# Routing the conversion of the first and second layers' weight chunks through PSUM, in a fused attention and two-layer MLP kernel

## The chip, the cores and the metric

One core of a Trainium2 chip runs the whole kernel in one launch. The metric is the device time of one execution in microseconds (us). The kernel before took 1555.38 us in the median of three runs (1552.1 to 1557.77).

## What is computed

Packed attention, then two gated MLPs one after the other, over 4608 tokens of width 512:

```
p_packed = softmax(scale * p @ k.T) @ v            # 32 packed rows per head
x  = softmax(scale * q @ p_packed.T) @ p_packed    # 8 batches, 8 heads, 576 tokens, head width 64
h  = x @ w_in;    x2  = (h * cos(h)) @ w_out       # 512 -> 2048 -> 512
h  = x2 @ w2_in;  out = (h * tanh(softplus(h))) @ w2_out
```

The four weight matrices arrive as 8-byte floats. The engines work on 4-byte ones, so each weight chunk of 128 rows by 512 columns is loaded as pairs of 4-byte words and put together on the chip.

## The kernel before, in words

The work runs in 16 token tiles of 288 tokens. Each tile goes through 16 steps, one per 128 columns of the hidden layer: 256 steps in all, then the second MLP in five blocks. In a step n (loop at line 911) the kernel traces, in this order: `l1(n)`, six TensorE matmuls that make a 128x288 piece of h in a PSUM bank; matmuls of background units; `l2(n-3)`, twelve matmuls into four accumulator banks; the chain h*cos(h), which is ScalarE's rounding (L802), VectorE's range reduction (L804), VectorE's clamp (L805), ScalarE's sine (L811), VectorE's product with h (L812, the last reader of the bank), ScalarE's rounding to the high half (L819) and GpSimd's low half (L822); and then VectorE, ScalarE and DMA work of background units, entered in tables by step (`at_pe`, `at_ew`, `at_ld`).

PSUM has eight banks. Four are the accumulators `acc0` to `acc3` (line 105), each with one buffer; they are first needed by `l2(0)`. Four are a ring (line 102) which `l1`, the folding of packed rows into the first layer's weights (`w_unit`, matmuls at L491, evacuation at L510 and L511), and the score and transpose banks of the attention share.

`conv` (line 408) converts a weight chunk. Its parts are: the load of the raw words (L424, on SP's queue); `c1`, in which ScalarE turns the high word into a scaled float (L436, a Prelu) and VectorE shifts the low word (L437); `c2`, in which VectorE merges the two (L441); `c3`, which writes the chunk to DRAM for later tiles (L446) or rounds the high half on ScalarE (L450); and `c4`, the low half on GpSimd (L455). All operands lie in SBUF. It serves three kinds of chunks: 16 of the first layer (`w_load`, line 462, placed at line 708 by `W0_STEP`, steps -5 to 10), 16 of the second layer's weights of the first MLP (`wo1_unit`, line 517, steps 0 to 15, with a raw buffer that is one of two), and 16 of the second MLP (`pre2`, much later).

A planner with its own costs of each instruction orders every engine's queue when the kernel is built. It goes by the order of tracing, by due times (`tc.high_priority`: l1 by 150, the chain by 200, the weight folding by 400) and by when it expects a buffer to be free. Each engine then executes its queue strictly in order.

Of the kernel before, what the change touches and what calls it, by code (L numbers as in the profile page):

```python
# [8 lines left out]
F32 = mybir.dt.float32  # L9
F32R = mybir.dt.float32r  # L10
I32 = mybir.dt.int32
AF = mybir.ActivationFunctionType
ALU = mybir.AluOpType
# [74 lines left out]
def build(tc, q, k, v, p, w1i, w1o, w2i, w2o, out):  # L88
    nc = tc.nc
    ctx = ExitStack()  # L90
    with ctx:
        wpool = ctx.enter_context(tc.tile_pool(name="wpool", bufs=1))
        psum = ctx.enter_context(tc.tile_pool(name="psum", bufs=1, space=bass.MemoryType.PSUM))
# [4 lines left out]
        def nm(s):  # L98
            cnt[0] += 1
            return f"{s}_{cnt[0]}"  # L100
# [3 lines left out]

        def accs():
            return [psum.tile([128, 512], F32, tag=f"acc{j}", bufs=1, name=nm(f"acc{j}")) for j in range(4)]

        def wo_tile(shape, dt):
            return wpool.tile(shape, dt, tag="wo", bufs=16, name=nm("wo"))

        def wab_tile(ab, shape, dt):
            return wpool.tile(shape, dt, tag="wa" if ab == 0 else "wb", bufs=4, name=nm("wab"))

        def ld_tile(shape):
            return wpool.tile(shape, F32, tag="ld", bufs=LD_BUFS, name=nm("ld"))
# [19 lines left out]
        def tmp_tile(shape):  # L135
            return tp.tile(shape, F32, tag="tmp", bufs=TMP_BUFS, name=nm("tmp"))
# [268 lines left out]
                (None, s7),  # L405
            ]

        def conv(src, shape, dst, save, wide=False, st=None):
            st = {} if st is None else st

            def load():
                if wide == "wo":
                    r = wo_tile([128, 512, 2], I32)
                elif wide:
                    w = wab_tile(1, [128, 2048], I32)
                    r = w[:, :1024].rearrange("p (f t) -> p f t", t=2)
                    st["t"], st["m"] = w[:, 1024:1536], w[:, 1536:].bitcast(F32)
                else:
                    r = tp.tile([128, 512, 2], I32, tag="raw", bufs=2, name=nm("raw"))
                n = shape[-1] if len(shape) == 3 else 512  # L420
                if len(shape) == 3:
                    nc.sync.dma_start(r.rearrange("p (a f) t -> p a (f t)", f=n), src.bitcast(I32))
                else:
                    ins = nc.sync.dma_start(r.rearrange("p f t -> p (f t)"), src.bitcast(I32))  # L424
                    last_w[0] = getattr(ins, "ins", ins)
                st["r"] = r

            def c1():
                r = st["r"]
                if wide == "wo":  # L430
                    w = wo_tile([128, 1024], I32)
                    st["t"], st["m"] = w[:, :512], w[:, 512:].bitcast(F32)
                elif not wide:
                    st["t"] = tp.tile([128, 512], I32, tag="tmp", bufs=TMP_BUFS, name=nm("cvt"))
                    st["m"] = tmp_tile([128, 512])
                nc.scalar.activation(st["m"], r[:, :, 1].bitcast(F32), AF.Prelu, scale=2.0**-112, alpha=2.0**32)  # L436
                nc.vector.tensor_scalar(st["t"], r[:, :, 0], 29, None, ALU.logical_shift_right)  # L437

            def c2():
                mi = st["m"].bitcast(I32)  # L440
                nc.vector.scalar_tensor_tensor(mi, mi, 3, st["t"], ALU.logical_shift_left, ALU.bitwise_or)  # L441

            def c3():
                if save is not None:
                    d = dram.tile([128, 512], F32, name=nm("ws"))
                    nc.sync.dma_start(d, st["m"])  # L446
                    save(d)
                if dst is not None:
                    hi, _ = st["x"] = dst()
                    nc.scalar.copy(hi, st["m"])  # L450

            def c4():
                if dst is not None:
                    hi, lo = st["x"]
                    nc.gpsimd.tensor_tensor(lo, st["m"], hi, ALU.subtract)  # L455

            return load, [c1, c2, c3, c4]

        W1 = {}
        w1s = {}  # L460

        def w_load(fg, hp, fresh=False):
            st = {}
            if fresh:
                load, cs = conv(
                    w1i[128 * hp : 128 * hp + 128, 512 * fg : 512 * fg + 512],
                    [128, 512],
                    None,
                    lambda d: w1s.__setitem__((fg, hp), d),
                    "wo" if fg == 0 else True,  # L470
                    st,
                )
                return st, load, cs[:-1]

            def load():
                st["m"] = ld_tile([128, 512])
                nc.sync.dma_start(st["m"], w1s[(fg, hp)])

            return st, load, []

        def w_unit(bs, fg, g, ms):
            st = {}

            def pe():
                for b in bs:
                    st[b] = ring()

                def head(b, l):
                    h = PERM[b % 2][l]
                    r = 64 * (h % 2)  # L490
                    return nc.tensor.matmul(  # L491
                        st[b][32 * l : 32 * l + 32],
                        PK[(b, g)][r : r + 64, 32 * l : 32 * l + 32],
                        ms[h // 2]["m"][r : r + 64],
                        start=True,
                        stop=True,
                    )

                todo = sorted(((b, l) for b in bs for l in range(4)), key=lambda x: (-(PERM[x[0] % 2][x[1]] // 2), -x[0]))
                ins = head(*todo[0])  # L500
                with tc.issue_after(getattr(ins, "ins", ins)), tc.high_priority(offset=HP_W):
                    for x in todo[1:]:
                        head(*x)

            def ew():
                for b in bs:
                    w = W1.get((b, fg))
                    if w is None:
                        w = W1[(b, fg)] = wab_tile(b % 2, [128, 2, 2, 512], F32R)
                    nc.scalar.copy(w[:, g, 0], st[b])  # L510
                    nc.vector.tensor_tensor(w[:, g, 1], st[b], w[:, g, 0], ALU.subtract)  # L511

            return pe, ew
# [3 lines left out]
        def wo1_unit(ft):  # L517
            def dst():
                w = wo_tile([128, 2, 512], F32R)
                WO[(1, ft)] = w  # L520
                return w[:, 0], w[:, 1]

            return conv(w1o[128 * ft : 128 * ft + 128, :], [128, 512], dst, None)

        WST = {}
        w2s = {}
# [1 line left out]
        def pre2(key, src, shape):  # L528
            return conv(src, shape, None, lambda d: w2s.__setitem__(key, d))
# [131 lines left out]
        def at_pe(n, f):  # L661
            bg_pe.setdefault(n, []).append(f)

        def at_ew(n, f):
            bg_ew.setdefault(n, []).append(f)

        def at_ld(n, f):
            bg_ld.setdefault(n, []).append(f)
# [37 lines left out]
        place(stages, [PRO + Q0_T + i for i in range(2)] + [PRO + Q0 + i for i in range(6)], HP_PRO)  # L706
        ms = {}
        for j in range(16):
            ms[j], load, cs = w_load(j // 4, j % 4, True)
            n = W0_STEP[j]  # L710
            at_ld(n - W0_LD if j >= 4 else PRO + W0E[j], load)
            for i, f in enumerate(cs):
                at_ew(n - 3 + i, f)
            if j % 2:
                pe, ew = w_unit((0,), j // 4, j % 4 // 2, (ms[j - 1], ms[j]))
                at_pe(n, pe)
                at_ew(n, ew)
        for ft in range(16):
            load, cs = wo1_unit(ft)
            n = ft + WO_OFF  # L720
            at_ld(n - 2, load)
            for i, f in enumerate(cs):
                at_ew(n + i // 2, f)
# [6 lines left out]
        for j in range(16):  # L730
            ms[j], load, _ = w_load(j // 4, j % 4)
            n = W01[0] + int(W01[1] * j)
# [12 lines left out]
        for j, n in enumerate(I_AT):  # L745
            w, c = divmod(j, 2)
            src = w2i[256 * c : 256 * c + 256, 256 * w : 256 * w + 256].rearrange("(a p) f -> p a f", p=128)
            load, cs = pre2((w, c), src, [128, 2, 256])
# [4 lines left out]
        for pair in range(3):  # L753
# [9 lines left out]
            for j in range(16):  # L763
                ms[j], load, _ = w_load(j // 4, j % 4)
                n = n0 + W_POS[pair][0] + int(W_POS[pair][1] * (j // 2 * 2 + 1))
# [5 lines left out]
        for t in range(1, NT):  # L771
            n = Q_N[t - 1]
# [52 lines left out]
        acc = {}  # L825

        def l2(n):
            t, s = divmod(n, NF)
            if s == 0:
                acc[t] = accs()  # L830
            w, gh = WO[(1, s)], hst[n]["gh"]
            for dc in range(4):
                o = 128 * dc
                mm3(acc[t][dc][:, :TT], w[:, 0, o : o + 128], w[:, 1, o : o + 128], gh[:, 0], gh[:, 1], s == 0, s == NF - 1)
            del hst[n]
# [75 lines left out]
        for n in range(NA + LAG_A):  # L911
# [7 lines left out]
            m = n - LAG_A  # L919
# [280 lines left out]
```

## Time and profile before

| what | value |
|---|---|
| median of 3 runs | 1555.38 us (1552.1 to 1557.77) |
| the profiled execution, its own time | 1555.48 us |
| its span, first to last instruction | 1552.9 us |
| mean granted TensorE clock | 0.989 of 2.4 GHz |
| busy: TensorE matmul, VectorE, ScalarE, GpSimd | 1475.9, 1117.8, 883.9, 639.2 us |
| DMA moved | 300.75 MB, mean 194 GB/s |

The table gives averages over the whole span. The span has parts with different limits, so the rows further down cut out the start of the kernel, where the weight chunks of the first MLP are converted. In the rows PE is TensorE, DVE VectorE, ACT ScalarE, POOL GpSimd and SP the queue that issues DMAs; L441 is line 441 of the kernel.

### The profile page before, as it was taken

The numbers are of one execution on the slowest core, as the hardware profiler recorded it, in microseconds if no ns is written. First come the engines' busy times: TensorE is split into PE (matmuls) and PEld (weight loads), VectorE is DVE, ScalarE is ACT, GpSimd is POOL, SyncE is SP. The second block draws the span as 40 slices with busy tenths as digits, with TensorE's granted clock in tenths as the row PEclk, the third lists the DMA queues.
The fourth block names the chain that finished last, engine by engine and source line by source line (L and its number), as shares of the span: only waits on it lengthen the run. The fifth ranks groups of instructions, "written<-read, shape, count | busy, mean of one in ns | idle before, by whom it ended". The sixth has DMA issues, their size and how long they took to land.

```text
span 1552.9 us, 28652 instructions
## 1 busy us (share of the span) xinstructions
PE 1475.9 (95%) x9728; PEld 1278.3 (82%) x9728; DVE 1117.8 (72%) x2082; ACT 883.9 (57%) x1838; POOL 639.2 (41%) x634
## 2 busy tenths in 40 slices
PE   3789999999999999999999999999999999999998
PEld 1567778788987898788999887888889898888997
DVE  4896666777776877678675878678668857766756
ACT  3675767666667677667665455344443534454443
POOL 0462333245643544627754666223522622352102
PEclk9899999999999999999999999999999999999999
DMA  9889676436648457533313767668868877877887
GB/s 293 283 214 226 170 184 161 123 101 176 186 122 225 139 152 195 163 107 104 104 49 98 259 217 241 193 196 242 266 212 235 298 223 219 244 205 221 241 257 202
DMA packets 247377, 300.75 MB, mean 194 GB/s; under 512 B 104384, under 2 KB 129472, under 8 KB 247232
## 3 DMA queue, kind: packets, MB, share of 16 engines
q1 hardware_dynamic: 246432, 298.73, 66.1%
q8 instruction: 77, 1.26, 0.3%
q14 instruction: 68, 0.56, 0.1%
q10 hardware_dynamic: 800, 0.20, 0.1%
HBM read 242.22 MB, written 56.62 MB: 192 GB/s over the span
## 4 chain that ended last, share of the span: by engine, by line
PE 50%; DVE 6%; ACT 3%; issue 2%; DMA 2%; POOL 1%; SPq 0%; DVEq 0%; ACTq 0%; POOLq 0%
PE acc L146 9%; PE acc L147 9%; PE acc L145 9%; PE ps L145 8%; PE ps L147 8%; PE ps L146 8%; DVE r L805 1%; ACT r L811 1%; DVE r L812 1%; DVE r L804 1%; DMA raw<-in_moe_w_in_dram 1%; DVE wab L897 1%; ACT wab L896 1%; PE ps L491 0%; DMA tst<-wt 0%
## 5 line engine op out<-in xcount | busy, mean ns | idle before, releaser
L822 POOL TENSOR_TENSOR gh<-r,gh 128x288 fp32r<-128x288 f32 x256 | 214.9, 847 | 334.3 <-ACT gh L819 231.7
L146 PE MATMUL acc<-gh,wo 128*128 128x288 f32 x1024 | 301.5, 301 | 2.2 <-POOL gh L822 1.7
L147 PE MATMUL acc<-gh,wo 128*128 128x288 f32 x1024 | 298.2, 298 | 0.0
L955 POOL TENSOR_TENSOR gh<-t,gh 128x512 fp32r<-128x512 f32 (+1 forms) x108 | 144.2, 1340 | 351.5 <-ACT gh L954 290.7
L145 PE MATMUL acc<-gh,wo 128*128 128x288 f32 x1024 | 273.7, 304 | 2.1 <-ACT gh L819 1.9
L145 PEld LDWEIGHTS acc<-gh,wo 128*128 128x128 f32 x1024 | 181.2, 190 | 34.6 <-issue 11.9
L146 PE MATMUL acc<-gh,T 128*128 128x512 f32 (+1 forms) x560 | 207.0, 371 | 2.2 <-DVE gh L955 1.7
L145 PE MATMUL ps<-wab,ws 128*128 128x512 f32 (+1 forms) x560 | 206.0, 369 | 1.8 <-ACT gh L954 0.8
L146 PEld LDWEIGHTS acc<-gh,wo 128*128 128x128 f32 x1024 | 194.1, 190 | 15.9 <-issue 9.5
L146 PE MATMUL ps<-wab,ws 128*128 128x512 f32 (+1 forms) x560 | 206.4, 369 | 0.0
L147 PE MATMUL ps<-wab,ws 128*128 128x512 f32 (+1 forms) x560 | 205.4, 369 | 0.0
L147 PE MATMUL acc<-gh,T 128*128 128x512 f32 (+1 forms) x560 | 205.1, 369 | 0.0
L147 PEld LDWEIGHTS acc<-gh,wo 128*128 128x128 f32 x1024 | 194.2, 190 | 5.8 <-issue 5.6
L955 DVE TENSOR_TENSOR gh<-wo,gh 128x512 fp32r<-128x512 f32 (+1 forms) x160 | 128.7, 810 | 81.7 <-ACT gh L954 81.3
L811 ACT ACTIVATE r<-r,halfpi 128x288 f32<-128x288 f32 x256 | 136.3, 535 | 83.9 <-DVE r L805 81.6
L145 PE MATMUL acc<-gh,T 128*128 128x512 f32 (+1 forms) x560 | 181.9, 369 | 0.6 <-DMA T<-tst 0.5
L145 PE MATMUL ps<-aT,wab 128*128 128x288 f32 x512 | 159.7, 312 | 22.7 <-DVE r L812 16.5
L812 DVE TENSOR_TENSOR r<-r,ps 128x288 f32<-128x288 f32 x256 | 114.5, 449 | 73.3 <-ACT r L811 72.5
L802 ACT ACTIVATE ki<-ps,quarter 128x288 int32<-128x288 f32 x256 | 125.1, 496 | 59.7 <-PE ps L147 49.6
L804 DVE SCALAR_TENSOR_TENSOR r<-ki,ps 128x288 f32<-128x288 int32 x256 | 113.8, 447 | 55.8 <-ACT ki L802 39.5
L146 PE MATMUL ps<-aT,wab 128*128 128x288 f32 x512 | 152.2, 297 | 0.0
L147 PE MATMUL ps<-aT,wab 128*128 128x288 f32 x512 | 151.5, 296 | 0.0
(169 smaller groups left out, 2956.1 us busy)
## 6 DMA issues: line engine op xcount, KB each, us to landing
T<-tst SPq DMA_DIRECT2D x280, 256.0 KB, 3.1
ws<-wst SPq DMA_DIRECT2D x224, 256.0 KB, 3.0
ld<-ws SPq DMA_DIRECT2D x80, 256.0 KB, 3.5
kr<-in_k_dram SPq DMA_DIRECT2D x64, 272.0 KB, 5.6
kr<-in_q_dram SPq DMA_DIRECT2D x60, 272.0 KB, 6.0
tst<-wt SPq DMA_DIRECT2D x56, 256.0 KB, 2.6
wst<-ws SPq DMA_DIRECT2D x56, 256.0 KB, 2.5
x2d<-xo SPq DMA_DIRECT2D x64, 144.0 KB, 1.8
```

What stands on the lines that cost most here:

```text
L145: nc.tensor.matmul(ps, l0, r0, start=first, stop=False, skip_group_check=more)
L146: nc.tensor.matmul(ps, l0, r1, start=False, stop=False, skip_group_check=more)
L147: nc.tensor.matmul(ps, l1, r0, start=False, stop=last, skip_group_check=more)
L802: nc.scalar.activation(ki, st["h"], AF.Identity, bias=quarter, scale=1.0 / TWO_PI)
L804: nc.vector.scalar_tensor_tensor(r, ki, -TWO_PI, st["h"], ALU.mult, ALU.add)
L805: (nc.gpsimd if n % C_MOD in C_POOL else nc.vector).tensor_scalar(r, r, 1.570796, -4.712388, ALU.min, ALU.max)
L811: nc.scalar.activation(g, g, AF.Sin, bias=halfpi, scale=1.0)
L812: nc.vector.tensor_tensor(g, g, st["h"], ALU.mult)
L822: nc.gpsimd.tensor_tensor(gh[:, 1], st["g"], gh[:, 0], ALU.subtract)
L896: nc.scalar.copy(x[:, a, 0, :n], src)
L897: (nc.gpsimd if k % 2 == 0 else nc.vector).tensor_tensor(x[:, a, 1, :n], src, x[:, a, 0, :n], ALU.subtract)
L955: eng.tensor_tensor(hl[:, 1, :n], src, hl[:, 0, :n], ALU.subtract)
```

## The change

`conv` gets an optional `bank`, a function that hands out a PSUM bank. Where it is given, ScalarE's Prelu writes into that bank in place of the SBUF tile, and the merge reads the bank and writes the SBUF tile. The first eight chunks of the first layer use the four accumulator banks in turn; the last eight, and all sixteen chunks of the second layer, use the ring. For the last eight chunks of the first layer, `c1` moves one step later, into the step of `c2`; `c2` and `c3` keep their steps. The second MLP's chunks stay in SBUF.

```diff
+        def acc_bank(j):
+            return lambda: psum.tile([128, 512], F32, tag=f"acc{j % 4}", bufs=1, name=nm("cb"))
...
-        def conv(src, shape, dst, save, wide=False, st=None):
+        def conv(src, shape, dst, save, wide=False, st=None, bank=None):
...
-                nc.scalar.activation(st["m"], r[:, :, 1].bitcast(F32), AF.Prelu, scale=2.0**-112, alpha=2.0**32)
+                st["p"] = bank() if bank else st["m"]
+                nc.scalar.activation(st["p"], r[:, :, 1].bitcast(F32), AF.Prelu, scale=2.0**-112, alpha=2.0**32)
...
-                mi = st["m"].bitcast(I32)
-                nc.vector.scalar_tensor_tensor(mi, mi, 3, st["t"], ALU.logical_shift_left, ALU.bitwise_or)
+                nc.vector.scalar_tensor_tensor(
+                    st["m"].bitcast(I32), st["p"].bitcast(I32), 3, st["t"], ALU.logical_shift_left, ALU.bitwise_or
+                )
...
-            return conv(w1o[128 * ft : 128 * ft + 128, :], [128, 512], dst, None)
+            return conv(w1o[128 * ft : 128 * ft + 128, :], [128, 512], dst, None, bank=ring)
...
-            ms[j], load, cs = w_load(j // 4, j % 4, True)
+            ms[j], load, cs = w_load(j // 4, j % 4, acc_bank(j) if j < 8 else ring)
...
-                at_ew(n - 3 + i, f)
+                at_ew(n - 3 + (i if j < 8 else i // 2 + 1), f)
```

## Rows read from the trace of the kernel before

**Rows 1.** The page's head.
```profile
span 1552.9 us, 28652 instructions
```
**Rows 2.** Stages: length, engines' busy us (count), granted clock, DMA share, GB/s.
```profile
50.00:112.00 62.00, 49.66 (x328) 40.41 (x329) 59.67 (x109) 46.88 (x91) 36.55 (x33) 0.86 0.86 249
...
140.00:700.00 560.00, 542.56 (x4615) 462.43 (x4606) 402.61 (x913) 383.04 (x827) 241.06 (x279) 0.99 0.59 159
700.00:1553.00 853.00, 839.36 (x4399) 746.00 (x4399) 611.49 (x958) 417.51 (x843) 346.86 (x306) 1.00 0.67 206
```
**Rows 3.** VectorE's costliest groups in 50 to 112 us: busy us, mean ns | idle before.
```profile
L441 DVE SCALAR_TENSOR_TENSOR tmp<-tmp,cvt 128x512 int32<-128x512 int32 x12 | 12.7, 1058 | 0.2
L441 DVE SCALAR_TENSOR_TENSOR wab<-wab 128x512 int32<-128x512 int32 x8 | 8.9, 1107 | 0.0
L805 DVE TENSOR_SCALAR r<-r 128x288 f32<-128x288 f32 x16 | 8.0, 507 | 0.0
...
L437 DVE TENSOR_SCALAR cvt<-raw 128x512 int32<-128x512 int32 x12 | 7.0, 582 | 0.0
L437 DVE TENSOR_SCALAR wab<-wab 128x512 int32<-128x512 int32 x8 | 5.3, 663 | 1.2 <-DMA wab<-in_moe_w_in_dram 1.2
```
**Rows 4.** Durations by line, ns shortest/median/longest; for L510 busy us and mean ns.
```profile
L441 DVE SCALAR_TENSOR_TENSOR tmp<-tmp,cvt x32: 645/692/1802, 42.6 to 690.0; 128x512 int32<-128x512 int32 x32
...
L511 DVE TENSOR_TENSOR wab<-ps,wab x7: 676/677/692, 45.1 to 93.0; 128x512 fp32r<-128x512 f32 x7
...
L812 DVE TENSOR_TENSOR r<-r,ps x19: 394/441/478, 54.3 to 124.3; 128x288 f32<-128x288 f32 x19
...
L436 ACT ACTIVATE wab<-wab x12: 652/664/690, 28.5 to 85.6; 128x512 f32<-128x512 f32 x12
...
L510 ACT CAST wab<-ps 128x512 fp32r<-128x512 f32 x9 | 5.1, 578 | 1.0 <-PE ps L491 1.0
```
**Rows 5.** Timeline: start us, us; two lengthened merges and a GpSimd instruction beside one.
```profile
51.69 1.78 DVE L441 SCALAR_TENSOR_TENSOR wab<-wab 128x512 int32<-128x512 int32 x1
...
109.22 1.80 DVE L441 SCALAR_TENSOR_TENSOR tmp<-tmp,cvt 128x512 int32<-128x512 int32 x1
...
51.66 1.26 POOL L455 TENSOR_TENSOR wo<-tmp,wo 128x512 fp32r<-128x512 f32 x1 [1.34 <-ACT wo L450]
```
**Rows 6.** Timeline: l1's first matmul and last read of its bank, steps 0, 11, 17, 24.
```profile
42.75 0.61 PE L145 MATMUL ps<-aT,wab 128*128 128x288 f32 x1
...
54.31 0.44 DVE L812 TENSOR_TENSOR r<-r,ps 128x288 f32<-128x288 f32 x1
...
92.56 0.29 PE L145 MATMUL ps<-aT,wab 128*128 128x288 f32 x1
...
99.03 0.43 DVE L812 TENSOR_TENSOR r<-r,ps 128x288 f32<-128x288 f32 x1
...
109.35 0.40 PE L145 MATMUL ps<-aT,wab 128*128 128x288 f32 x1 [0.35 <-DVE r L812]
...
117.73 0.46 DVE L812 TENSOR_TENSOR r<-r,ps 128x288 f32<-128x288 f32 x1 [0.45 <-ACT r L811]
...
140.09 0.40 PE L145 MATMUL ps<-aT,wab 128*128 128x288 f32 x1
...
144.01 0.46 DVE L812 TENSOR_TENSOR r<-r,ps 128x288 f32<-128x288 f32 x1 [0.66 <-ACT r L811]
```
**Rows 7.** Timeline: one chunk's Prelu and merge; one weight folding's matmuls and last read.
```profile
81.44 0.66 ACT L436 ACTIVATE wab<-wab 128x512 f32<-128x512 f32 x1
...
84.74 1.39 DVE L441 SCALAR_TENSOR_TENSOR wab<-wab 128x512 int32<-128x512 int32 x1
...
86.28 1.93 PE L491 MATMUL ps<-wab,pk 64*32 64x512 f32 x8 [3.77 <-DVE wab L441]
...
89.59 0.68 DVE L511 TENSOR_TENSOR wab<-ps,wab 128x512 fp32r<-128x512 f32 x1
```
**Rows 8.** Timeline: the merge of the eighth first-layer chunk.
```profile
35.32 1.05 DVE L441 SCALAR_TENSOR_TENSOR wab<-wab 128x512 int32<-128x512 int32 x1 [0.51 <-ACT wab L510]
```

More of the change, by code (lines that the diff above doesn't have):

```diff
@@ L460, in build, with w_load @@
         w1s = {}
-        def w_load(fg, hp, fresh=False):
+        def w_load(fg, hp, fresh=None):
             st = {}
@@ L471, in w_load @@
                     st,
+                    fresh,
                 )
```

## The prediction

> **What bounds the kernel now.** I first cut the span into stages, because the share of busy time over the whole of it hides them. From 140 us on TensorE is the limit: its matmuls are busy 542.56 of 560 us and 839.36 of 853 us, at a granted clock of 0.99 to 1.00 [rows 2]. So a microsecond gained or lost before 140 us moves the end by a microsecond. In the stretch from 50 to 112 us it is otherwise. VectorE is busy 59.67 of 62 us, TensorE 49.66 us at a mean granted clock of 0.86 (a mix of its two levels, 1.2 and 2.4 GHz), ScalarE 46.88, GpSimd 36.55, and the DMA engines have 0.86 of their time taken [rows 2]. VectorE sets the pace there, and this is the stretch in which nearly all weight chunks are converted.
>
> Next I looked at what VectorE does in it. The merges of chunk halves (L441) are its costliest group: 12.7 + 8.9 = 21.6 us in 20 instructions, 1.08 us each [rows 3], while the shortest merge takes 0.645 us and the longest 1.802 [rows 4]. The same instruction on the same shape is lengthened up to 2.8 times. The timeline shows beside what: the merge at 51.69 us took 1.78 us, and GpSimd's L455 had begun at 51.66 and ran 1.26 us [rows 5]. Both read and write SBUF; the merge's end is the end of GpSimd's instruction plus about the merge's own time. Now compare VectorE's instructions with one operand in PSUM: L511 takes 676 to 692 ns and L812 394 to 478 ns through the same stretch, beside the same GpSimd instructions [rows 4]. They are never lengthened.
>
> **The sum goes against the profiled execution:** 1555.48 us, a span of 1552.9 [rows 1] and 2.6 us around it. It lies 0.1 us over the median shown, so the result is compared with the median as it stands.
>
> **The change, part by part.**
>
> *Merges.* After the change a merge has one operand in a bank, as L511 has, on the same 128x512 shape. I price it at 0.68 us [rows 4]. The 20 merges of the stretch then cost 13.6 us in place of 21.6: 8.0 us less. Not all of it stays. Twelve of the 20 are lengthened beyond 0.8 us. Seven of these are followed at once by a shift or a clamp (L437, L805), which are lengthened in the same way: their means of 582, 663 and 507 ns [rows 3] lie well over what the unhindered ones take. There the rest of the wait goes to the next instruction. What is saved then is at most the merge's own 0.68 us, which now runs beside GpSimd: instead of 4.3 us of lengthening over the seven, 3.4. The other five are followed by instructions that read a bank or are tiny, and keep their 3.7 us, as the one at 109.22 us [rows 5]. That makes 7.1 us. GpSimd's 36.55 us also fall into a shorter stretch, from a share of 0.59 to 0.65, so the lengthening of the 36 shifts and clamps, about 7 us over unhindered 0.41 and 0.30 us, grows by a tenth, 0.7 us. VectorE's part comes to **-6.4 us**: 62 becomes 55.6. The bounds are 8.0 (nothing displaced) and 3.7 (all seven displaced in full).
>
> The row says that a bank as a source costs the merge nothing: 677 ns (L511) against a median of 692 for SBUF alone. The Trainium skill, in "VectorE: DVE Perf Modes", section on the TRN2 errata, gives VectorE a fixed term of 120 cycles from PSUM and 58 from SBUF, which would make each merge 65 ns dearer. By that estimate the sum would be 1.3 us smaller over the 20. I go by the row.
>
> *Prelu into a bank.* No row shows ScalarE writing to PSUM. From above it costs what it does into SBUF, 664 ns, from below the 578 ns of L510, which reads a bank of the same size [rows 4]: 0 to 1.7 us of ScalarE over the 20. ScalarE is not the pace-setter, and I take 0. A cost above 664 ns I allow by the same 1.7 us.
>
> *First eight chunks.* Their banks are the accumulators. The last of these merges ended by 36.4 us [rows 8], and the second layer's first product needs the chain of step 0, whose product ended at 54.75 us [rows 6]. Some 18 us of cover: cost nothing. Little is gained either, as GpSimd hardly works then.
>
> *Chunks 8 to 15, first part one step later.* It issues one Prelu and one shift, no DMA; the merge and the store to DRAM keep their steps, so neither SP's queue nor GpSimd's is passed. The raw words lie in the tile of the whole chunk, so no buffer comes free later. Cost 0; a step there is some 4 us, and should the merge be late for it, the folding at L491 waits, as it does now for 3.77 us [rows 7].
>
> *The ring.* This is the new wait. Twenty conversions in the stretch each take one of four banks from Prelu to merge. In the order of before that is 4.7 us for the chunk at 81.44 us [rows 7]; over the 20 I read a mean of 3.4, or 3.0 with the merges at 0.68: 60 bank-us. The folding and attention banks take about 60 more (one folding held its bank 4.0 us [rows 7]; there are five, two banks of one query tile and two of one key unit). And l1 holds a bank from its first matmul to the product: 12.0 us in step 0, 8.8 in step 17 [rows 6], 152 us inside the stretch over these 18, some 9.5 for each of 16 steps. Four banks over 62 us are 248. With holds as now the ring would need 152 + 60 + 60 = 272, or 68 us: more than it has. But the hold is largely queueing at VectorE and shrinks with it: 6.9 us in step 11 and 4.4 in step 24, out of the jam [rows 6]. I take 6.6, nearest to step 11, as it is still in the jam. The ring then needs (16 x 6.6 + 120) / 4 = **56.4 us**. That is a little over VectorE's 55.6, so it sets the end: 62 - 56.4 = 5.6 us gained.
>
> What is queued behind a Prelu that waits for a bank: ScalarE's rounding and sine of the running chains, so VectorE's next product; and the raw buffer (one of two for second-layer chunks), so SP's next raw load and the key and query loads behind it. Behind an l1 that waits are the second layer's matmuls.
>
> Sum: 1555.48 - 5.6 = 1549.9, said as **1550.0 us**. A change under 0.3% (4.7 us) can hardly be told from none here.
>
> **The rivals.**
>
> *A. The ring becomes the bound, slower.* Place: Prelu and l1 both wait for a bank between 50 and 112 us. For it: l1 is seen to wait for the product of an earlier step already now (the releaser named in the row at 109.35) [rows 6], and 272 exceeds 248. Against it: holds shrink when VectorE has less to do. It decides from a hold of (248 - 120) / 16 = 8.0 us: above, the stretch gets longer than 62. With today's 9.5 it takes 68, so +6.0: 1561.5 us. The Trainium skill warns in the same direction ("ScalarE: Activation LUTs", step-by-step section): writing to PSUM is the quicker way out of ScalarE, but useful only if TensorE doesn't need most of PSUM. Here all eight banks have users; no run yet shows which half of that weighs more.
>
> *B. VectorE's time is freed but mostly not used.* The items on its queue wait for loads (the shifts waited 1.2 us for one chunk [rows 3]; DMA share 0.86) and for chains of five engines' steps, and the planner's order stays as tight as before. A third of the gain is left, 2 us: 1553.5 us. For: ScalarE and TensorE, with their 46.88 and 49.66 us, are not far behind. Against: VectorE idles only 2.3 us in 62 now.
>
> *C. The change doesn't do what it says:* the merge still has the shifted low word and its output in SBUF, and is lengthened as before; nothing is gained, the banks cost a little: 1556.5 us. Against: L511 and L812 also have one operand and the output in SBUF [rows 4].
>
> **How the numbers follow.** Forecast 0.55, A 0.20, B 0.20, C 0.05. The forecast's own range runs from 1543.5 (8.0 us of merges, 1.7 of Prelus, 2 for the order of a re-planned queue) to 1553. Of its 0.55 I count 0.47 below 1550.7 and 0.08 within 0.3%. B and C lie within. A lies over 1560 with 0.17 and within with 0.03. So faster 0.47, same 0.36, slower 0.17. The range goes from the forecast's lower end to most of A: 1543.5 to 1560.5.
>
> **What would show it.** Right: merges (now two lines in the source) at about 0.68 us without long ones; VectorE's busy time of the conversion stretch down by 6 us, and the second layer's first tile done 5 to 6 us earlier; shifts and clamps a little longer in the mean. Rival A: Prelus whose releaser is a product (L812) or merge, and l1 waiting longer than now. B: VectorE idle in the stretch, with loads or ScalarE as releasers. C: merges still up to 1.8 us. The forecast is wrong if the stretch isn't shortened although the merges are, or if the time after 140 us changes by more than a microsecond or two.

## The result, and the profile after

The changed kernel takes 1570.28 us in the median of six runs against 1554.62 for the kernel before: a ratio of 1.0097, with a 95% interval of 1.0080 to 1.0114. It is slower by 15 to 16 us, where 5.4 us less were forecast, and beyond rival A's 1561.5. The profiled execution took 1569.45 us, its span is 1567.7.

The first view is the one by stages (length, busy us of TensorE, its weight loads, VectorE, ScalarE, GpSimd, then granted clock, DMA share, GB/s), to be held against [rows 2].

```profile
50.00:112.00 62.00, 44.93 (x243) 33.04 (x244) 46.08 (x88) 39.76 (x75) 26.17 (x24) 0.78 0.75 228
...
140.00:700.00 560.00, 541.90 (x4612) 460.72 (x4612) 397.50 (x907) 381.96 (x828) 238.16 (x276) 1.00 0.60 160
700.00:1553.00 853.00, 845.20 (x4491) 752.49 (x4489) 615.74 (x974) 428.14 (x860) 350.86 (x313) 1.00 0.67 206
```

From 140 us on TensorE is the limit as before. In the stretch from 50 to 112 us every engine is busy for less time than before, and so are the DMA engines. No engine has become the bound. They wait for each other, and fewer instructions were done (243 TensorE matmul records where there were 328). TensorE's granted clock is lower too, 0.78 where it was 0.86.

The second view groups the merge (L444 now) and the Prelu (L440) by duration, shortest/median/longest in ns, as [rows 4] do.

```profile
L444 DVE SCALAR_TENSOR_TENSOR tmp<-ps,cvt x16: 652/677/692, 45.0 to 127.2; 128x512 int32<-128x512 int32 x16
L444 DVE SCALAR_TENSOR_TENSOR tmp<-tmp,cvt x16: 668/692/1289, 241.1 to 707.7; 128x512 int32<-128x512 int32 x16
L444 DVE SCALAR_TENSOR_TENSOR wab<-ps,wab x8: 672/683/692, 52.5 to 94.6; 128x512 int32<-128x512 int32 x8
...
L440 ACT ACTIVATE ps<-raw x16: 612/634/651, 44.3 to 123.7; 128x512 f32<-128x512 f32 x16
L440 ACT ACTIVATE tmp<-raw x16: 660/672/712, 240.2 to 704.4; 128x512 f32<-128x512 f32 x16
```

The change does what it says. A merge that reads a bank takes 692 ns at most, while those of the second MLP's chunks, still in SBUF, reach 1289. The Prelu into a bank is about 40 ns quicker than into SBUF.

Where the time went is seen by following the steps. This table gives the first matmul of l1 in us, worked out from the timeline of TensorE, and when the last store of the first tile's output and of the sixteenth's was issued.

| kernel | step 2 | step 4 | step 8 | step 16 | first tile stored | step 64 | tile 16 stored |
|---|---|---|---|---|---|---|---|
| before | 46 | 57 | 77 | 106 | 126 | 278 | 845 |
| changed | 53 | 64 | 91 | 127 | 144 | 296 | 863 |

All of the loss arises before the first tile is stored: 7 us by step 2, 14 by step 8, 21 by step 16, 18 at the end of the tile. It then stays at 18 for the other fifteen tiles. Some 3 us are given back in the second MLP; no run here says why.

Not all of the 18 us is waiting. These two rows, in the columns of [rows 2], run from the first l1 to the l1 of step 32, first in the kernel before and then in the changed one:

```profile
42.75:167.40 124.65, 105.85 (x824) 84.49 (x821) 100.36 (x207) 89.27 (x177) 56.70 (x52) 0.91 0.90 240
44.55:185.72 141.17, 115.37 (x819) 88.47 (x816) 96.29 (x208) 90.56 (x179) 53.96 (x53) 0.88 0.81 213
```

The changed kernel takes 16.5 us more. TensorE is idle for 7.0 of them (25.8 in place of 18.8 us). For the other 9.5 it is busy longer with nearly the same number of matmuls. Part of that is its clock. The granted 0.88 and 0.91 are means of the two levels, 1.2 and 2.4 GHz; by them TensorE had the lower level for 34 us in place of 22. Twelve more microseconds at half the clock cost 6 of the 9.5 us at most, by this estimate. No run separates the rest.

The third view is the timeline of four queues at two places of the changed kernel (start us, us; in brackets the idle time before, and its releaser).

```profile
47.05 0.81 SPq L427 DMA_DIRECT2D wab<-in_moe_w_in_dram  x2
...
51.85 0.64 ACT L440 ACTIVATE ps<-wab 128x512 f32<-128x512 f32 x1 [4.15 <-DMA wab<-in_moe_w_in_dram]
...
52.53 0.69 DVE L444 SCALAR_TENSOR_TENSOR wab<-ps,wab 128x512 int32<-128x512 int32 x1 [0.31 <-ACT ps L440]
...
53.37 0.58 PE L148 MATMUL ps<-aT,wab 128*128 128x288 f32 x1 [4.18 <-DVE wab L444]
...
85.11 0.33 SPq L427 DMA_DIRECT2D wab<-in_moe_w_in_dram  x1
...
89.53 0.66 ACT L440 ACTIVATE ps<-wab 128x512 f32<-128x512 f32 x1 [2.10 <-DMA wab<-in_moe_w_in_dram]
...
90.22 0.69 DVE L444 SCALAR_TENSOR_TENSOR wab<-ps,wab 128x512 int32<-128x512 int32 x1 [0.19 <-ACT ps L440]
...
91.06 0.37 PE L148 MATMUL ps<-aT,wab 128*128 128x288 f32 x1 [0.69 <-DVE wab L444]
```

Read each group of four from the bottom. The l1 of step 2 at 53.37 us needs a ring bank. The bank belongs to first-layer chunk 8, so l1 waits for that chunk's merge. The merge waits for the Prelu, and the Prelu waited 4.15 us for the chunk's load. In the kernel before the l1 of step 2 began seven microseconds earlier, as this row of it shows:

```profile
46.35 0.29 PE L145 MATMUL ps<-aT,wab 128*128 128x288 f32 x1
```

Chunk 8 itself is no later in the changed kernel: its merge ended at 53.47 us before [rows 5] and ends at 53.22 now. What is new is that l1 stands behind it. The same chain is seen at step 8, at 91.06 us, though there l1 itself waited only 0.69 us for its bank.

The waits of the stretch from 20 to 150 us (total us, times, longest) show the loads as releasers.

```profile
DVE wab L441 <- DMA wab<-in_moe_w_in_dram: 8.6, 4, 3.4
...
ACT ps L440 <- DMA wab<-in_moe_w_in_dram: 6.3, 2, 4.2
...
PE ps L148 <- DVE wab L444: 4.9, 2, 4.2
...
PE ps L148 <- DVE tmp L444: 4.1, 2, 3.6
```

So l1 waits 9.0 us in all for merges of chunks. In the kernel before it waits for none in the same stretch.

And the holds of l1 did not shrink. In step 11 it is 11.1 us now, from the first matmul to the end of the product, where it was 6.9 [rows 6]:

```profile
103.55 0.61 PE L148 MATMUL ps<-aT,wab 128*128 128x288 f32 x1
...
114.18 0.44 DVE L818 TENSOR_TENSOR r<-r,ps 128x288 f32<-128x288 f32 x1
```

Over the first sixteen steps the holds add up to 159 us in both kernels, 9.9 us each. The conversions, on the other hand, hold a bank only briefly: from the start of the Prelu to the end of the merge the 24 of the ring take 56 us together, 2.3 us each (worked out from the timelines of ScalarE and VectorE).

### The profile page after: what moved, and what is told of

It reads as the page before. It is cut to its first block, busy times and chain, and to the rows that moved or that the text cites. A ratio compares the mean times of both kernels' runs of the same rounds, so it can differ in the third digit from the quotient of the medians.

```text
span 1567.7 us, 28650 instructions
## 1 busy us (share of the span) xinstructions
PE 1483.1 (95%) x9728; PEld 1282.1 (82%) x9728; DVE 1109.4 (71%) x2082; ACT 886.5 (57%) x1838; POOL 633.1 (40%) x634
## 4 chain that ended last, share of the span: by engine, by line
PE 51%; DVE 5%; ACT 2%; DMA 2%; issue 1%; POOL 1%; SPq 0%; DVEq 0%; ACTq 0%; POOLq 0%
PE acc L149 9%; PE acc L148 9%; PE acc L150 9%; PE ps L148 8%; PE ps L149 8%; PE ps L150 8%; DVE r L811 1%; ACT r L817 1%; DVE r L818 1%; DVE r L810 1%; DMA raw<-in_moe_w_in_dram 1%; PE ps L497 0%; DMA raw<-in_moe_w_out_dram 0%; DMA ws<-wst 0%; ACT wab L902 0%
## 5 line engine op out<-in xcount | busy, mean ns | idle before, releaser
L818 DVE TENSOR_TENSOR r<-r,ps 128x288 f32<-128x288 f32 x256 | 114.2, 448 | 70.3 <-ACT r L817 69.6
```

The source lines that it names most:

```text
L818: nc.vector.tensor_tensor(g, g, st["h"], ALU.mult)
```

## The experiments

Every run was timed beside the kernel before on the same chip; ratios are against it, as its own median went from 1554.84 to 1557.45 us in these timings. The names stand for: *R*, too few ring banks; *T*, banks that wait for loads; *H*, banks that are held, whatever for; *P*, another order of the queues by the planner; *L* and *M*, the late chunks and their moved step; *V*, VectorE's time paces the first tile; *W*, loads, chains and banks pace it.

**Is a ring bank worth that much?** The kernel before with three banks.

```diff
-            return psum.tile([128, 512], F32, tag="ps", bufs=4, name=nm("ps"))
+            return psum.tile([128, 512], F32, tag="ps", bufs=3, name=nm("ps"))
```

> The kernel before with three ring banks in place of four, conversions in SBUF as they were. Theory R (the ring): the changed kernel is slow because its 24 conversions take about one of four ring banks away from l1, the folding and the attention share while the first tile runs. Then taking one bank away with nothing else changed must cost a like amount or more, since here it is missing for good: 1565 to 1580 us, most of it before the first tile's end. Theory P (the plan): the banks are not short; the changed kernel is slow because the planner laid the queues in another order and because of the part moved one step. Then three banks cost little: under 1560 us.

Measured: 1637.07 us, ratio 1.0521 (1.0504 to 1.0539). That is far over the range, since every tile pays; the sixteenth is stored at 925 us, 79 later. The first tile alone is stored at 137 us, 11 later. So a bank missing for good costs the first tile 11 us, less than the change's 18. By the start of step 16 the two are closer, 17 us late against 21 in the profiled executions. A bank is worth much, and this run alone doesn't rule R out.

**One part of the change at a time.** First the first eight chunks in accumulator banks alone, then the second layer's chunks in the ring alone, then chunks 8 to 15 in the ring alone, then nothing but the moved step.

```diff
# e2_first8 (where it gets True, conv stays in SBUF)
-            ms[j], load, cs = w_load(j // 4, j % 4, True)
+            ms[j], load, cs = w_load(j // 4, j % 4, acc_bank(j) if j < 8 else True)
# e3_second
-            return conv(w1o[128 * ft : 128 * ft + 128, :], [128, 512], dst, None)
+            return conv(w1o[128 * ft : 128 * ft + 128, :], [128, 512], dst, None, bank=ring)
# e4_late8, and its last two lines alone in e5_move
-            ms[j], load, cs = w_load(j // 4, j % 4, True)
+            ms[j], load, cs = w_load(j // 4, j % 4, True if j < 8 else ring)
-                at_ew(n - 3 + i, f)
+                at_ew(n - 3 + (i if j < 8 else i // 2 + 1), f)
```

> Only the first eight chunks go through PSUM, in the accumulator banks that nobody uses yet; all others as before. Theory R: no ring bank is taken and these merges are hardly lengthened before, so 1553 to 1557 us. Theory P: a re-planned start alone shifts loads and foldings; 1560 us or more would speak for it.

> Only the 16 chunks of the second layer go through the ring; the first layer's chunks and their steps as before. Theory R: 16 of the 24 ring takers, so about two thirds of the 15 us: 1562 to 1567 us. Rival L (the late first-layer chunks and their moved part, which the foldings wait for, make the loss): under 1559 us here.

> Only chunks 8 to 15 of the first layer go through the ring, with their first part one step later as in the change; the first eight and the second layer as before. Theory R: 8 of the 24 ring takers, about a third: 1558 to 1562 us. Rival L: most of the loss, 1565 us or more.

> Only the step of the first part of chunks 8 to 15 moves, as in the change; all conversions stay in SBUF as before. Theory R (ring banks taken by conversions are the cost): nothing happens, 1552 to 1559 us. Rival M (the move makes the loss of the run with the late eight chunks alone, 8 us): 1561 to 1566 us.

| run | us | ratio | 95% interval |
|---|---|---|---|
| first eight alone | 1559.04 | 1.0019 | 1.0003 to 1.0035 |
| second layer alone | 1565.14 | 1.0059 | 1.0038 to 1.0080 |
| chunks 8 to 15 alone | 1564.81 | 1.0048 | 1.0032 to 1.0064 |
| the move alone | 1555.78 | 0.9997 | 0.9981 to 1.0012 |

The moved step costs nothing, so rival M falls. Both ring parts come out slower. But they don't go by their number of chunks: eight first-layer chunks, at 1.0048, cost nearly as much as sixteen second-layer ones, at 1.0059. That speaks against R in its plain form, so much per bank taken, but weakly: the intervals just reach the third and the two thirds of the loss that it wants, 1.0032 and 1.0065. The first eight alone may cost 3 us at 1.0019, though their banks are in nobody's way. Nor does l1 wait for a single merge in either of the two ring runs. With the second layer alone it waits longer for the chains' products, 15.1 us where it was 8.9 (this run, then the kernel before, from 20 to 150 us):

```profile
PE ps L148 <- DVE r L818: 15.1, 5, 6.5
...
PE ps L145 <- DVE r L812: 8.9, 6, 6.2
```

The 7 to 9 us of each of these two runs are thus not traced to a chunk's load.

**Holding a bank without waiting for anything, and with.** The conversion goes back to SBUF. Each chunk only takes the bank that the change gives it: ScalarE writes 8 columns ahead of the Prelu, VectorE reads them ahead of the merge, each at its place in its engine's queue. In the second of these runs the 8 columns come from the loaded chunk.

```diff
+                    st["b"] = bank()
# e6_hold
+                    nc.scalar.copy(st["b"][:, :8], hold)
# e10_hold_load
+                    nc.scalar.copy(st["b"][:, :8], r[:, :8, 1].bitcast(F32))
...
+                    nc.vector.tensor_copy(junk, st["b"][:, :8])
```

> The changed kernel, but conversions run in SBUF as before; each only holds the bank that the change gives it: ScalarE writes 8 columns into it ahead of the Prelu and VectorE reads them ahead of the merge (some 0.2 and 0.1 us more for each of 32 chunks). Theory R: holding is the cost, so at least as slow as the changed kernel, 1568 to 1580 us, with the merges lengthened as before. If the cost lies in what the Prelu and the merge do in a bank: under 1562 us.

> The run that only holds the banks, with one difference: the 8 columns that ScalarE writes into the bank come from the loaded chunk, so a bank can't be given back before that chunk's load has landed. Theory T (a bank that waits for a load: the conversions put the weight loads into the chain that l1 and the foldings wait for): the loss of 9 us grows to that of the changed kernel, 1566 to 1573 us. Rival H (holding alone, whatever it waits for; the rest comes from the Prelu and the merge working in a bank): 1560 to 1565 us.

Measured: 1564.47 us, ratio 1.0044 (1.0025 to 1.0063), for holding alone; 1569.86 us, ratio 1.0090 (1.0062 to 1.0119), where the held bank waits for its load. The first was expected at 1568 at least and comes to less than half of the loss. The second comes near the changed kernel's 1.0097, in T's range and over H's; the two intervals just touch. The edits differ by a single operand, a constant tile or the chunk's raw words, and by what the planner makes of it. The Prelu and the merge needn't touch the bank at all. The time of holding isn't what tells the two apart: from copy to read the 24 ring banks are held 2.0 us in the mean in the first run and 1.4 in the second (from the timelines). In the second run's profiled execution, at 1572.81 us, the first tile is stored 11 us late, not 18; some 6 more are lost after it. The first run's is one of its fastest, 1558.16 us. The timeline of the second run shows the same chain as the changed kernel, at the same place (L449 is VectorE's read of the held bank):

```profile
50.32 0.17 ACT L443 COPY ps<-wab 128x8 f32<-128x8 f32 x1 [2.76 <-DMA wab<-in_moe_w_in_dram]
...
50.91 0.37 PE L149 MATMUL ps<-aT,wab 128*128 128x288 f32 x1 [2.83 <-DVE gap_a L449]
```

l1 waits for a held bank which waits for a load. With the one that only holds, l1 of step 2 begins at 47.97 us, 2.9 earlier.

**What is a shorter merge worth by itself?** The kernel before, with GpSimd's subtraction for second-layer chunks replaced.

```diff
-                    nc.gpsimd.tensor_tensor(lo, st["m"], hi, ALU.subtract)
+                    nc.gpsimd.memset(lo.bitcast(F32), 0.0)
```

> The kernel before; the low half of every converted second-layer chunk is left out: GpSimd fills it with zeros, which reads nothing, in place of the subtraction. Merges then should be lengthened less, with no bank taken: the gain that the change was to bring, by itself. Theory V (VectorE's busy time sets the pace of the first tile, as the prediction had it): 1545 to 1550 us. Rival W (the first tile is paced by loads, chains and banks, and VectorE's lengthened merges fill time that would be waited away): 1553 to 1558 us.

Measured: 1559.46 us, ratio 1.0017 (0.9997 to 1.0038): no gain, and a little over W's range. VectorE did get its relief, as its busy time in the stretch shows, against 59.67 [rows 2]; and the first tile is stored at 121 us, 5 us early. The granted clock of the stretch is higher too, 0.92 against 0.86, so the 5 us need not all be VectorE's. But then, from 112 to 140 us, TensorE loses it again. These are this run's stages, in the columns of [rows 2], and two rows of its timeline:

```profile
50.00:112.00 62.00, 50.32 (x345) 41.51 (x342) 55.28 (x113) 49.54 (x98) 23.54 (x30) 0.92 0.86 255
112.00:140.00 28.00, 21.35 (x182) 17.86 (x184) 14.69 (x41) 15.97 (x35) 4.94 (x7) 0.95 1.06 237
```

```profile
135.94 0.31 DVE L206 STREAM_TRANSPOSE pp<-pc 128x128 f32<-128x128 f32 x1 [4.91 <-DMA pc<-in_p_dram]
...
137.09 0.61 PE L145 MATMUL ps<-aT,wab 128*128 128x288 f32 x1 [3.06 <-DVE r L812]
```

The kernel before has 24.31 us of TensorE in the same 28 us, at a DMA share of 1.09, by this stage row of it; the second row is the same transposition there:

```profile
112.00:140.00 28.00, 24.31 (x207) 20.59 (x206) 16.44 (x44) 18.21 (x40) 6.54 (x8) 0.94 1.09 244
...
136.78 0.30 DVE L206 STREAM_TRANSPOSE pp<-pc 128x128 f32<-128x128 f32 x1
```

There the packed rows and keys of the second batch are loaded, with the DMA engines' time full in both kernels. VectorE's queue stands 4.91 us for one of these loads, the running chain's product stands behind it, and the next l1 waits 3.06 us for that product's bank. The load let the transposition begin at 135.94 us, where it ran at 136.78 in the kernel before: an earlier first tile hardly brought it forward. At step 24 both kernels are at 140 us. Theory V, by which this run should have gained 5 us or more, falls for this kernel.

**Lighter loads.** Each second-layer chunk is loaded by half, and the half converted twice: the kernel before, the same with the low halves left out, and the changed kernel.

```diff
-                    ins = nc.sync.dma_start(r.rearrange("p f t -> p (f t)"), src.bitcast(I32))
+                    ins = nc.sync.dma_start(r[:, :256].rearrange("p f t -> p (f t)"), src[:, :256].bitcast(I32))
```

> The kernel before, where each of the 16 second-layer chunks is loaded by half (256 of 512 columns, 4 MB less in all) and the half is converted twice, with instructions of the same size. Theory W (the weight loads pace the first tile): 1543 to 1550 us. If the loads have slack: 1553 to 1558 us.

> Halved loads as in the run beside it, and the low halves left out (zeros from GpSimd). If VectorE's lengthened merges are the next limit once loads have slack (V): 3 to 6 us under the run with halved loads alone. If not: within 2 us of it.

> The changed kernel with the same halved loads. Theory T: loads land earlier, banks come back earlier, and the loss against the kernel before with halved loads falls from 15 us to under 9. Theory R (too few banks, whatever they wait for): the loss stays at 12 to 16 us.

| run | us | ratio | 95% interval |
|---|---|---|---|
| before, halved loads | 1560.57 | 1.0034 | 1.0015 to 1.0053 |
| and low halves left out | 1563.46 | 1.0050 | 1.0030 to 1.0070 |
| changed, halved loads | 1563.27 | 1.0052 | 1.0035 to 1.0069 |

Halving these loads doesn't speed up the kernel before; it comes out 6 us slower, outside both ranges. Its step 3 begins at 61.39 us in place of 54.81, after a wait for a folded weight (L518) that the kernel before doesn't have. So nothing speaks for the second layer's loads as what paces the first tile (W in that form), and shorter merges don't pay with lighter loads either (V falls again). The loss of the changed kernel over the kernel before, with the same halved loads in both, is 1563.27 - 1560.57 = 2.7 us in place of 15. That is T's side of the fork, but it is not the proof it seems to be, since the base has a wait of its own. At the end of the first tile the loss between these two is still 7 us (stored at 129.6 and 136.6). And the waits of l1 for merges have not shrunk with the lighter loads: 14.2 us where the changed kernel has 9.0. These are the rows from 20 to 150 us, the first of the kernel before with halved loads, the others of the changed kernel with them (L451 is the merge):

```profile
PE ps L145 <- DVE wab L518: 7.9, 1, 7.9
...
PE ps L148 <- DVE wab L451: 10.0, 3, 6.0
...
PE ps L148 <- DVE tmp L451: 4.2, 3, 2.1
```

What can be said is that lighter loads made the changed kernel faster, from 1.0097 to 1.0052 with intervals apart, and the kernel before not. By which wait they did is not shown.

**Can the holds be shortened, or the loads be had early enough?** First l1 without its due time in the first 18 steps; then the ring conversions planned a step later.

```diff
# e8_l1_late
-                with tc.high_priority(offset=HP_L1):
+                with tc.high_priority(offset=HP_L1 if n >= 18 else 0):
# e16_later_second; e15_later has this, and i // 2 + 2 for chunks 8 to 15
-                at_ew(n + i // 2, f)
+                at_ew(n + 1 + i // 2, f)
```

> The changed kernel with l1 of the first 18 steps planned at its place in the order of tracing, without its due time 150 earlier. It tests the step of the prediction in which l1's hold of a bank shrinks. If the hold (10 us in the first 16 steps) is made by l1's earliness, it falls to 5 to 7 us and the loss shrinks: 1556 to 1563 us. If the hold is the chain's own time in queues that are executed in order, it stays near 10 us and nothing is won: 1567 us or more.

> The changed kernel with all ring conversions planned one step (some 4 to 5 us) later: chunks 8 to 15 and the second layer's. Theory T: a bank is asked for when the load has landed, so it is held for the conversion alone; 1557 to 1565 us, near the run that holds banks without waiting for loads. If lateness isn't it, or the foldings and the second layer now wait for the later conversions: 1568 us or more.

> The same for the second layer's chunks alone; chunks 8 to 15 stay as in the change. Theory T: part of the loss comes back, 1562 to 1567 us. Otherwise 1568 us or more.

| run | us | ratio | 95% interval |
|---|---|---|---|
| l1 without its due time | 1569.75 | 1.0080 | 1.0053 to 1.0107 |
| all ring conversions later | 1568.36 | 1.0069 | 1.0048 to 1.0089 |
| second layer's alone later | 1566.38 | 1.0062 | 1.0038 to 1.0086 |

Without its due time l1 holds its bank for 10.0 us in the mean of the first 16 steps: the hold is not made by l1's earliness. Planning conversions later wins back about a third, and the intervals overlap with the changed kernel's; the run with the second layer's alone lies in T's range, the other in that of the opposite reading. The waits went elsewhere. With all conversions later, step 8 starts at 83 us (changed: 91, before: 77), but then the second layer's products wait for its own late weights, four times and 4.2 us in all, as in the first and last of these rows (L455 rounds the high half of a converted chunk); l1 still waits for merges, as in the middle one:

```profile
75.57 0.40 PE L148 MATMUL acc<-gh,wo 128*128 128x288 f32 x1 [2.18 <-ACT wo L455]
...
82.57 0.61 PE L148 MATMUL ps<-aT,wab 128*128 128x288 f32 x1 [2.01 <-DVE wab L444]
...
90.43 0.40 PE L148 MATMUL acc<-gh,wo 128*128 128x288 f32 x1 [1.45 <-ACT wo L455]
```

**Banks that nobody needs.** Only accumulator banks, for the first eight chunks and the first three of the second layer.

```diff
+            ..., dst, None, bank=acc_bank(ft) if ft < 3 else None)
```

> Only accumulator banks are used: for the first eight first-layer chunks and the first three second-layer chunks; all others stay in SBUF, steps as before. No ring bank is taken. Theory T with W (VectorE's merges don't pay): 1553 to 1559 us. If merges in a bank pay where no ring bank is taken: under 1551 us.

Measured: 1563.6 us, ratio 1.0039 (1.0021 to 1.0056), over the range. At step 16 this kernel is at 107 us, a microsecond behind the kernel before. The loss comes after it, past the last merge of the first MLP's chunks at 109.71 us:

```profile
114.26 0.31 DVE L209 STREAM_TRANSPOSE pp<-pc 128x128 f32<-128x128 f32 x1 [3.43 <-DMA ld<-in_v_dram]
...
120.20 1.13 PE L256 MATMUL ps<-ident,tmp 128*128 128x128 f32 x4 [5.60 <-ACT tmp L241]
```

VectorE's queue stands 3.43 us for a load of the second batch, and a transpose of that batch's key unit waits 5.60 us for its exponentials. The profiled execution, at 1558.91 us, is the fastest of its ten, so it need not show all of the loss. None of the runs points to a version that beats the kernel before.

## Why the prediction was wrong, point by point

**What bounds the kernel.** From 140 us on TensorE is the limit and a loss is carried to the last tile in full: right, 18 us at the first tile's end and at the sixteenth's. That a gain in the stretch from 50 to 112 us is still there at 140 was wrong in the one run that tests it. With the low halves left out VectorE had 4.4 us less to do in the stretch (59.67 - 55.28) and the first tile was stored 5 us early; by step 24, behind loads of the second batch, nothing was left of it. "VectorE sets the pace" read a busy share of 96% as a bound. It was one for the first tile at most. The prediction's own sign of being wrong came true: the merges are shortened and the stretch is not. The clock had no term in the sum; it went from 0.86 to 0.78 in the stretch, where TensorE now stands idle for 17.1 us in place of 12.3.

**Merges.** Priced at 0.68 us, measured medians 677 to 686: right. The 32 merges of the first MLP's chunks take 21.8 us in place of 30.1, 8.3 less. Part went over to the clamp, as foreseen: from 40 to 125 us its median is 882 ns (L811 now), where the unhindered 0.30 us had been the common case, and its mean rose by some 0.31 us, 5.0 us for 16. The shifts got cheaper by 0.14 us each, 3.5 us for 25. Together that is 1.5 us, near the 1.6 that the prediction took off. The rule of "VectorE: DVE Perf Modes" in the Trainium skill (section on the TRN2 errata), a dearer fixed term from PSUM, does not show on this instruction: the merge from a bank is, if anything, 10 ns quicker than the median of 692 from SBUF. To go by the row was right.

**Prelu.** 0 was taken, within 1.7 us either way. Measured medians are 633 to 643 ns against 664 to 676: some 0.03 us less each. The size was of no account.

**First eight chunks, cost nothing.** Not quite. Alone they come to 1.0019, at the edge of what can be told. The prediction misread the order here. The merge in [rows 8] is that of the eighth chunk, but not the last of the eight: chunk 3, which is loaded late, was merged at 40.19 us in the kernel before (the first row). That leaves 14 us of cover, not 18. And four accumulators serve eight chunks, so chunk 7 needs the bank of chunk 3. Its Prelu in the changed kernel has the second row, and its merge ran at 43.91 us where it was 35.32:

```profile
40.19 0.65 DVE L441 SCALAR_TENSOR_TENSOR wo<-wo 128x512 int32<-128x512 int32 x1
...
42.67 0.64 ACT L440 ACTIVATE cb<-wab 128x512 f32<-128x512 f32 x1 [1.03 <-DVE wo L444]
```

**The moved step, cost 0.** Right: 0.9997.

**The ring, the step that failed.** The prediction took the hold of l1 at 6.6 us, since it "shrinks" with VectorE's load, and priced the ring by bank-time alone. The hold stayed at 9.9 us. With that, its own formula gives (16 x 9.9 + 120) / 4 = 69.6 us for the stretch, 7.6 more; with the 9.5 that it read inside the stretch it gave 68, 6 more, which was rival A. But rival A's price was too low too, by a factor of 2 to 3, because it counted how long a conversion holds a bank and not what the holder waits for. The size of that hold was not the fault: 3.0 us were taken and 2.3 measured. Of A's two signs one appeared: l1 waits longer for its banks, 15.7 us from 20 to 150 us where it was 8.9. The other did not: the ring's Prelus wait for loads, 6.3 us in all, and not for a product or a merge. The prediction had the pieces apart: it named the raw loads behind a waiting Prelu, and in rival B the shifts that wait for loads. It did not join them. A bank given to a conversion ties l1 to that chunk's load; this the rows of step 2 show. The Prelu and the folding free the buffers into which SP loads the next chunks, and so the next load can be late as well. In the changed kernel the loads of chunks 8 and 9 go out from 47.05 us on, where they went from 44.9, and the last raw chunk at 115 us where it was 103, both read from SP's timeline. Its loads wait 7.3 us for foldings between 40 and 125 us, where they waited 1.7 in the kernel before:

```profile
SPq L427 <- PE ps L497: 7.3, 3, 3.1
...
SPq L424 <- PE ps L491: 1.7, 1, 1.7
```

Held banks alone gave 1.0044; with the held bank waiting for its load it is 1.0090, near the whole loss.

One sum of the prediction is off: its lower end, 1555.48 less 8.0, 1.7 and 2, is 1543.8 and not 1543.5. Nothing hung on it.

The caveat that rival A cited from "ScalarE: Activation LUTs" in the Trainium skill (step-by-step section), that PSUM as a destination is only useful if TensorE doesn't need most of it, agrees with the result: the Prelu gets some 40 ns quicker and the kernel 15 us slower.

**What stays open.** How much of the smaller losses is the planner's. Kernels that take no ring bank but are planned anew came out between 0.9997 and 1.0050, none faster than before. The 1.0044 of holding alone, and the 1.0048 and 1.0059 of the two ring parts, are hardly more, so it is not shown that holding ring banks without waiting for a load costs anything by itself, and theory P has a share that these runs don't measure. The step from 1.0044 to 1.0090 is no larger than that spread and could contain some of it as well. What stands in the timeline, in the changed kernel and in the run whose held banks wait, is l1 behind a bank that waits for a load. So it is shown that l1 inherits such waits, that ring banks for conversions go with the loss, and that the moved step doesn't. It is not shown how the 15 us divide among the waits for loads, the new order of the queues and TensorE's longer busy time at a lower clock. A run with the order of the queues kept as in the kernel before would be needed for that. The 3 us given back in the second MLP were not looked into.

## What to carry to other kernels

Before a step is moved into a shared ring of banks, ask not only how long it will hold one but what stands ahead of it: the user that gets the bank next inherits that wait, here for weight loads that l1's matmuls of that step had nothing to do with. A bank is better asked for after the load has landed, though planning for that won back only a third here. And a busy share near 1 in one stretch does not make a saving there worth its size: look at what the next stretch is waiting for, here loads at a full DMA share.

## What the runs showed of the hardware

- VectorE's merge of two SBUF tiles is lengthened beside GpSimd's work to as much as 1802 ns [rows 4]; with one operand in PSUM none of 32 takes over 692 ns. Part of the wait then shows at an instruction with all operands in SBUF: the clamp's median in the jam went from 298 ns, by the source view of the kernel before from 40 to 125 us, to 882.
- ScalarE's Prelu writes 128x512 floats into a PSUM bank in 634 ns and into SBUF in 672, from the same kind of raw tile (medians of 16 each, in the changed kernel).
- For nearly the same matmuls TensorE was busy 115.37 us at a mean granted clock of 0.88 and 105.85 at 0.91.
- One PSUM bank of four less in the matmuls' ring costs this kernel 5.2%.
